# A linear-attention plus MoE kernel on one core: a new ramp, decays one unit earlier, and k and r transposed by the DMA

## The chip, the core and the metric

The kernel runs on one core of a Trainium2 chip. The metric is device time in microseconds (us) of the slowest core, here the only one. The engines are TensorE (PE in the profile, PEld for its weight loads), VectorE (DVE), ScalarE (ACT), GpSimd (POOL) and SyncE (SP), which here issues every DMA. Each engine executes its own instructions in the order in which the program gives them to it, as the traces show.

The kernel before has a median of 236.32 us over its first 3 runs (235.04 to 237.77).

## The reference, cut to what matters

The inputs r, k, v and w have the shape (4 batches, 8 heads, 768 steps, 48), in float32. The first part is a recurrence with a decaying state; the second is a dense layer pair with a gelu between.

```python
for t in range(S):                        # S = 768
    cur = einsum('bhd,bhe->bhde', u[None] * kt, vt)
    y[:, :, t] = einsum('bhd,bhde->bhe', rt, state + cur)
    state = wt[:, :, :, None] * state + einsum('bhd,bhe->bhde', kt, vt)
x = y.transpose(0, 2, 1, 3).reshape(B * S, H * D)      # 3072 x 384
h = x @ w_in                                           # 384 x 2048
g = 0.5 * h * (1 + tanh(c * (h + 0.044715 * h**3)))
out = g @ w_out                                        # 2048 x 384
```

## The kernel before

The work is cut into 12 units: 3 windows of 256 time steps times 4 batches. Inside a window the recurrence becomes matmuls. The logarithms of w are summed with triangular matrices on TensorE (`a1`), ScalarE takes exponentials of the sums (`exps`), VectorE multiplies k and r by them (`kk`, `rq`), and both products are transposed (`a2`) because the next matmuls contract over the head dimension. The term with u needs the row sum of r·k·u (`rk`, `dg`, `vsc`). Then the dense layer pair (called MoE in the program and below) runs on the unit's 256 rows (`mm1`, `mm2`). The attention of unit q+1 is woven into the MoE of unit q, and the preparation of unit q+2 follows it.

```python
def prep(q):                                    # cut
    DVE.tensor_tensor(out=kk[:, :, :, 0:D], in0=tdh(kt), in1=dec(e1), op=AL.mult)
    DVE.tensor_tensor(out=rq[:, :, :, 0:D], in0=tdh(rt), in1=dec(fq), op=AL.mult)
    POOL.tensor_copy(out=vb, in_=tdh(vt))
    POOL.tensor_tensor(out=rk, in0=kt..., in1=rt..., op=AL.mult)
    POOL.tensor_tensor(out=rk, in0=rk, in1=u_bc..., op=AL.mult)
    ...

def a2(q, which):
    src = (kk, rq)[which]
    for g in range(G):
        for t2 in range(2):
            PE.transpose(ps[:, g, :, t2, :], src[:, t2, ds(2 * g, 2), :], ident)
    DVE.tensor_copy(out=dst, in_=ps)

for q in range(NU):                             # the main loop, cut
    if q + 3 < NU:
        for nm in ("k", "r", "v"):
            load(q + 3, nm)                     # at the top, needed by prep(q+3) a unit later
    if q + 4 < NU:
        load(q + 4, "w")
    ...                                         # mm1, mm2, attention(q+1), a1(q+2)
    exps(q + 2)
    ln(q + 3)
    mm2(q, 0, range(12, 16))
    store(q, 0)
    prep(q + 2)
    prep_b(q + 2)
    mm2(q, 1, ...)
    store(q, 1)
```

In unit 0 the weights of w_out are cast to bfloat16 as well: all eight casts are placed before the first `mm2` and before most of the attention of unit 1.

Of the kernel before, what the change touches and what calls it, by code (L numbers as in the profile page):

```python
# [19 lines left out]
def kernel(  # L20
# [15 lines left out]
    P = 128  # L36
# [90 lines left out]
    kk_ps = [pfix.tile([P, 2, H, 64], BF, name=f"kk{i}") for i in range(2)]  # L127
    rq_ps = [pfix.tile([P, 2, H, 64], BF, name=f"rq{i}") for i in range(2)]
# [19 lines left out]

    st = {}
# [10 lines left out]
    def ln(q):  # L160
        lw = logws[q % 3]
        ACT.activation(  # L162
            out=lw[:, :, :, 0:D].rearrange("p t h d -> p h t d"),
            in_=ld.pop(("w", q)).rearrange("p h (t d) -> p h t d", t=2), func=AF.Ln)

    def a1(q):
        lw = logws[q % 3]
        x, y, z = (ps_a.tile([P, 512], FP, tag="a", name=f"cum{q}_{i}") for i in range(3))
        for dst, s0, s1 in ((x, strict, strict), (y, incl, strict), (z, incl, incl)):
            PE.matmul(dst[:, 0:HD], s0, lw[:, 0, :, 0:D], start=True, stop=False)  # L170
            PE.matmul(dst[:, 0:HD], s1, lw[:, 1, :, 0:D], start=False, stop=True)  # L171
        for g in range(G):
            for t2 in range(2):
                PE.matmul(z[:, ds(HD + 2 * g, 2)], lw[:, t2, ds(2 * g, 2), :], ones2,
                          start=False, stop=(t2 == 1), skip_group_check=True)
        st["cum", q] = (x, y, z)

    def exps(q):
        x, y, z = st.pop(("cum", q))
        fq = pw2.tile([P, 2, HD], BF, tag="fq", name=f"fq{q}")  # L180
        e1 = pw2.tile([P, 2, HD], BF, tag="e1", name=f"e1{q}")
        al = pw2.tile([P, G, 2], FP, tag="al", name=f"al{q}")
        ACT.activation(out=e1[:, 0, :], in_=y[:, 0:HD], func=AF.Exp, scale=-1.0)
        ACT.activation(out=e1[:, 1, :], in_=z[:, 0:HD], func=AF.Exp, scale=-1.0)
        ACT.activation(out=fq[:, 0, :], in_=x[:, 0:HD], func=AF.Exp)
        ACT.activation(out=fq[:, 1, :], in_=y[:, 0:HD], func=AF.Exp)
        ACT.activation(out=al, in_=z[:, ds(HD, 2 * G)].rearrange("p (g c) -> p g c", c=2),  # L187
                       func=AF.Exp)
        st["dec", q] = (fq, e1, al)

    def prep(q):
        fq, e1, al = st.pop(("dec", q))
        kt, rt, vt = ld.pop(("k", q)), ld.pop(("r", q)), ld.pop(("v", q))
        kk, rq = kk_ps[q % 2], rq_ps[q % 2]

        def tdh(ap):
            return ap.rearrange("p h (t d) -> p t h d", t=2)

        def dec(ap):
            return ap.rearrange("p t (h d) -> p t h d", h=H)  # L200

        DVE.tensor_tensor(out=kk[:, :, :, 0:D], in0=tdh(kt), in1=dec(e1), op=AL.mult)
        DVE.tensor_tensor(out=rq[:, :, :, 0:D], in0=tdh(rt), in1=dec(fq), op=AL.mult)  # L203
        vb = pw2.tile([P, 2, H, D], BF, tag="vb", name=f"vb{q}")
        POOL.tensor_copy(out=vb, in_=tdh(vt))
        rk = pw2.tile([P, H, 2, D], FP, tag="rk", name=f"rk{q}", bufs=1)
        dg = pw2.tile([P, H, 2], FP, tag="dg", name=f"dg{q}")
        vsc = pw2.tile([P, 2, H, D], BF, tag="vsc", name=f"vsc{q}")
        am = pw2.tile([P, 2, G, 2 * D], FP, tag="am", name=f"am{q}")
        POOL.tensor_tensor(out=rk, in0=kt.rearrange("p h (t d) -> p h t d", t=2),  # L210
                           in1=rt.rearrange("p h (t d) -> p h t d", t=2), op=AL.mult)
        POOL.tensor_tensor(out=rk, in0=rk,  # L212
                           in1=u_bc[:, :, None, :].broadcast_to([P, H, 2, D]), op=AL.mult)
        for c2 in range(2):
            POOL.tensor_tensor(  # L215
                out=am[:, c2], in0=blk.rearrange("p g j d -> p g (j d)"),
                in1=al[:, :, c2][:, :, None].broadcast_to([P, G, 2 * D]), op=AL.mult)
        st["pre", q] = (kk, rq, vb, vsc, am)
        st["diag", q] = (rk, dg)

    def prep_b(q):
        kk, rq, vb, vsc, am = st["pre", q]
        rk, dg = st.pop(("diag", q))
        DVE.tensor_reduce(out=dg, in_=rk, axis=AX.X, op=AL.add)
        POOL.tensor_tensor(
            out=vsc, in0=vb,
            in1=dg.rearrange("p h t -> p t h")[:, :, :, None].broadcast_to([P, 2, H, D]),
            op=AL.mult)

    def a2(q, which):  # L230
        kk, rq, vb, vsc, am = st["pre", q]
        src = (kk, rq)[which]
        ps = ps_a.tile([P, G, 2, 2, 64], BF, tag="a", name=f"T{q}_{which}")
        for g in range(G):
            for t2 in range(2):
                PE.transpose(ps[:, g, :, t2, :], src[:, t2, ds(2 * g, 2), :], ident)  # L236
        dst = pw2.tile([P, G, 2, 2, 64], BF, tag=f"T{which}", name=f"TT{q}_{which}")
        DVE.tensor_copy(out=dst, in_=ps)  # L238
        st["T", q, which] = dst

    def a3(q, rnd):
        kT, rT = st["T", q, 0], st["T", q, 1]
        mts = [ps_a.tile([P, 2, 2, P], FP, tag="a", name=f"mt{q}_{rnd}_{j}") for j in range(2)]
        for gi in range(2):
            g = 2 * rnd + gi
            for t2 in range(2):
                for j in range(2):
                    for c2 in range(2):
                        PE.matmul(mts[j][ds(64 * c2, 64), gi, t2, :],
                                  kT[ds(64 * j, D), g, c2, t2, :],  # L250
                                  rT[ds(64 * j, D), g, c2, :, :],
                                  start=(gi + t2 == 0), stop=(gi + t2 == 2))
# [8 lines left out]
    def a4(q):  # L261
        wi, b = units[q]
        kk, rq, vb, vsc, am = st["pre", q]
# [10 lines left out]
        for t2 in range(2):  # L274
            for c2 in range(2):
                rows = ds(64 * c2, 64)
                PE.matmul(ys[c2][:, :, :],
                          sel.rearrange("p a b t -> p a (b t)")[rows, t2, :],
                          vsc[rows, t2, :, :], start=False, stop=False,
                          skip_group_check=True)  # L280
        st["y", q] = ys

    def a4p(q):
        wi, b = units[q]
        kk, rq, vb, vsc, am = st["pre", q]
# [3 lines left out]
        for g in range(G):  # L289
            for t2 in range(2):  # L290
                for c2 in halves:
                    rows = ds(64 * c2, 64)
                    PE.matmul(p2[c2][:, g, :], kk[rows, t2, ds(2 * g, 2), :],
# [17 lines left out]
    def a5(q, c2):  # L311
        ys, rT = st["y", q], st["T", q, 1]
        s = st.pop(("S", q, c2))
        for g in range(G):
            if s is not None:
                PE.matmul(ys[c2][:, ds(2 * g, 2), :], rT[:, g, c2, :, :], s[:, g, :],
# [7 lines left out]
    def a6(q):  # L324
        xs = st.pop(("xs", q))
        ps = ps_a.tile([P, NCB, 2, P], BF, tag="a", name=f"xTp{q}")
        for c2 in range(2):
            for cb in range(NCB):
                PE.transpose(ps[:, cb, c2, :], xs[:, c2, ts(cb, P)], ident)
        xT = pw2.tile([P, NCB, WIN], BF, tag="xT", name=f"xT{q}")  # L330
        DVE.tensor_copy(out=xT, in_=ps.rearrange("p a b t -> p a (b t)"))
# [5 lines left out]
    def mm1(q, i):  # L337
# [4 lines left out]
        for f in range(2):  # L342
            ft = 2 * i + f
            for cb in range(NCB):
                PE.matmul(h[:, f, :], w_in_sb[:, cb, ts(ft, P)], xT[:, cb, :],  # L345
# [25 lines left out]
    def attention(q):  # L371
        a2(q, 1)
        a2(q, 0)
        yield
# [13 lines left out]

    for i in range(6):
        load_w_in(i)  # L390
    for nm in ("k", "r", "v"):
        load(1, nm)
# [6 lines left out]
    for nm in ("k", "r", "v"):  # L399
        load(2, nm)  # L400
# [3 lines left out]
    a1(0)  # L404
    exps(0)
    prep(0)
    ln(1)
    att = attention(0)
    next(att)
    next(att)  # L410
    next(att)
    prep_b(0)
    next(att)
    cast_w_in(0, ACT)
    cast_w_in(1, ACT)
    cast_w_in(2, DVE)
    next(att)
    next(att)
    next(att)
    cast_w_in(3, ACT)  # L420
    cast_w_in(4, POOL)
    cast_w_in(5, DVE)
    a1(1)
    exps(1)
    prep(1)
    prep_b(1)

    for q in range(NU):
        if q + 3 < NU:
            for nm in ("k", "r", "v"):  # L430
                load(q + 3, nm)
        if q + 4 < NU:
            load(q + 4, "w")
        att = attention(q + 1) if q + 1 < NU else iter(())
        table("gelu")
        ramp = q < 2
        if ramp:
            for i in range(8):
                mm1(q, i)
            if q == 0:  # L440
                for i in range(8):
                    cast_w_out(i, DVE if i in (0, 3, 6) else (ACT if i in (1, 4, 7) else POOL))
        for i in range(8):
            if not ramp:
                mm1(q, i)
            if i >= 2:
                mm2(q, 0, (2 * i - 4, 2 * i - 3))
            if i in (1, 3, 4, 5, 6, 7):
                next(att, None)
            if i == 6 and 0 < q and q + 2 < NU:  # L450
                a1(q + 2)
        table("exp")
        if q == 0:
            ln(2)
            a1(2)
        if q + 2 < NU:
            exps(q + 2)
        if q + 3 < NU:
            ln(q + 3)
        mm2(q, 0, range(12, 16))  # L460
        if not ramp:
            for _ in att:
                pass
        store(q, 0)
        if q + 2 < NU:
            prep(q + 2)
            prep_b(q + 2)
        mm2(q, 1, range(8))
        for _ in att:
            pass  # L470
        mm2(q, 1, range(8, 16))
        store(q, 1)

# [29 lines left out]
```

## Time and profile before

I measure a unit from the first MoE matmul of one unit (`h_0`) to that of the next, as the timeline shows them. "Start" is the time up to the first of them.

| us | start | unit 0 | 1 | 2 | 3 | 4 to 8 | 9, 10 | last | sum |
|---|---|---|---|---|---|---|---|---|---|
| before | 24.78 | 28.96 | 20.30 | 17.30 | 16.57 | 82.15 | 30.58 | 15.26 | 235.9 |

The page of the kernel before gives the busy time and share of each engine, then, for 40 equal slices of the span, the busy tenths of TensorE and the clock that it was granted (PEclk, in tenths of full speed).

```profile
span 235.9 us, 5759 instructions
...
PE 203.4 (86%) x2448; PEld 143.0 (61%) x2448; DVE 131.3 (56%) x211; ACT 134.0 (57%) x223; POOL 104.5 (44%) x87
...
PE   0456787598895999999999999999999999999992
...
PEclk9999996779997999999999999999999999999998
```

From about the fourteenth slice on, TensorE has no slack. Before that there is a ramp in which it is idle for part of most slices, and its clock falls to 0.6 or 0.7 in some of them.

The view of busy time by stretch shows the same for the start, unit 0 and a steady unit. Columns: the stretch, its length, busy us and instruction count of each engine, granted clock, DMA share (above 1 in some stretches, so not used here), GB/s.

```profile
core 0: us, PE busy (x) PEld busy (x) DVE busy (x) ACT busy (x) POOL busy (x), PEclk, DMA share, GB/s
0.00:24.78 24.78, 11.34 (x138) 7.68 (x139) 16.05 (x41) 9.32 (x14) 11.07 (x20) 1.00 1.04 294
24.78:53.74 28.96, 21.54 (x210) 13.49 (x207) 19.95 (x21) 16.41 (x27) 18.43 (x14) 0.82 0.80 212
124.47:141.03 16.56, 15.89 (x210) 11.42 (x208) 10.18 (x17) 10.51 (x20) 8.22 (x6) 1.00 0.54 121
```

In the steady unit TensorE is busy 15.89 of 16.56 us. VectorE is at 10.2, so there is room on every other engine.

The timeline of VectorE and GpSimd in unit 0 of the kernel before:

```profile
42.50 0.56 DVE L304 TENSOR_TENSOR tmp_1_642<-p_1_622,S_0_639 128x384 f32<-128x384 f32 x1
43.14 1.80 POOL L212 TENSOR_TENSOR rk_696<-rk_696,u_bc 128x768 f32<-128x768 f32 x1
43.16 2.20 DVE L305 TENSOR_TENSOR S_1_641<-tmp_1_642,am_421 128x384 bf16<-128x384 f32 x1
```

Two VectorE operations of the same shape follow each other. The first takes 0.56 us; the second, which reads two tiles from SBUF, the memory on the chip that the engines share, while a GpSimd instruction runs, takes 2.20 us and ends at 45.36, which is 0.42 us after the GpSimd instruction ended (44.94).

### The profile page before, as it was taken

How to read it: one execution, taken by the hardware profiler on the slowest of the kernel's cores; microseconds unless marked ns; L12 is line 12 of the kernel's file. 1: busy time of each engine (PE TensorE's matmuls, PEld its weight loads, DVE VectorE, ACT ScalarE, POOL GpSimd, SP SyncE). 2: the span in 40 equal slices, each digit the busy share in tenths (PEclk: the TensorE clock that was granted, in tenths of full speed). 3: DMA queues.
4: the chain of work that ended last, by engine and by line, in shares of the span. 5: the costliest groups of instructions: out<-in, count | busy, mean ns of one | idle time of the engine just before them, and what ended most of it. 6: DMA issues, size and time to landing. Idle time of an engine off the chain costs nothing.

```text
span 235.9 us, 5759 instructions
## 1 busy us (share of the span) xinstructions
PE 203.4 (86%) x2448; PEld 143.0 (61%) x2448; DVE 131.3 (56%) x211; ACT 134.0 (57%) x223; POOL 104.5 (44%) x87
## 2 busy tenths in 40 slices
PE   0456787598895999999999999999999999999992
PEld 0334564357564767667767667676777677677761
DVE  7684686561636538547547747656285376374200
ACT  3433780566255449459368377395494684765670
POOL 3473792639008504806708509329158076060000
PEclk9999996779997999999999999999999999999998
DMA  7999999713902911942923914915719120020202
GB/s 173 307 396 297 331 320 255 160 33 72 231 15 54 246 25 36 206 98 53 232 56 75 257 24 111 210 33 124 182 35 212 24 62 10 13 56 0 68 1 67
DMA packets 56969, 30.45 MB, mean 129 GB/s; under 512 B 50928, under 2 KB 56176, under 8 KB 56944
## 3 DMA queue, kind: packets, MB, share of 16 engines
q1 hardware_dynamic: 56944, 30.09, 52.1%
q8 instruction: 19, 0.31, 0.6%
q14 instruction: 6, 0.05, 0.1%
HBM read 25.36 MB, written 4.72 MB: 127 GB/s over the span
## 4 chain that ended last, share of the span: by engine, by line
PE 54%; ACT 19%; DVE 11%; issue 9%; POOL 3%; DMA 2%; DVEq 0%; ACTq 0%; POOLq 0%
ACT L156 5%; DVE w_out_sb L86 2%; DMA w_89<-in_w_dram 2%; PE o_0_532 L354 1%; DVE rq_127 L203 1%; ACT logw_124 L162 1%; PE o_0_3678 L354 1%; PE o_0_3457 L354 1%; PE o_0_3175 L354 1%; PE o_1_3740 L354 1%; PE o_1_3632 L354 1%; PE o_1_3389 L354 1%; POOL rk_418 L210 1%; POOL rk_418 L212 1%; ACT logw_122 L162 1%
## 5 line engine op out<-in xcount | busy, mean ns | idle before, releaser
L345 PEld LDWEIGHTS <-w_in_sb 128*128 128x128 bf16 x576 | 54.0, 99 | 21.1 <-issue 9.9
L156 ACT ACT_TABLE_LOAD x13 | 16.7, 1283 | 0.9 <-PEq L487 0.7
L158 ACT ACT_TABLE_LOAD x12 | 15.4, 1283 | 0.2
L171 PEld LDWEIGHTS <-strict 128*128 128x128 bf16 x24 | 2.5, 104 | 9.9 <-issue 9.5
L215 POOL TENSOR_TENSOR am_997<-blk,al_975 128x384 f32<-128x384 bf16 x2 | 2.4, 1230 | 12.5 <-ACT al_975 L187 12.5
L215 POOL TENSOR_TENSOR am_1304<-blk,al_1273 128x384 f32<-128x384 bf16 x2 | 2.4, 1229 | 11.5 <-ACT al_1273 L187 11.5
L215 POOL TENSOR_TENSOR am_1608<-blk,al_1577 128x384 f32<-128x384 bf16 x2 | 2.4, 1230 | 8.3 <-ACT al_1577 L187 8.3
L215 POOL TENSOR_TENSOR am_1912<-blk,al_1881 128x384 f32<-128x384 bf16 x2 | 2.4, 1230 | 8.3 <-ACT al_1881 L187 8.3
L215 POOL TENSOR_TENSOR am_2216<-blk,al_2185 128x384 f32<-128x384 bf16 x2 | 2.4, 1230 | 8.3 <-ACT al_2185 L187 8.3
L215 POOL TENSOR_TENSOR am_2520<-blk,al_2489 128x384 f32<-128x384 bf16 x2 | 2.4, 1228 | 8.3 <-ACT al_2489 L187 8.3
L215 POOL TENSOR_TENSOR am_2811<-blk,al_2780 128x384 f32<-128x384 bf16 x2 | 2.4, 1228 | 7.9 <-ACT al_2780 L187 7.9
L215 POOL TENSOR_TENSOR am_3100<-blk,al_3069 128x384 f32<-128x384 bf16 x2 | 2.4, 1228 | 7.9 <-ACT al_3069 L187 7.9
L215 POOL TENSOR_TENSOR am_3382<-blk,al_3352 128x384 f32<-128x384 bf16 x2 | 2.4, 1228 | 7.9 <-ACT al_3352 L187 7.9
L354 PE MATMUL o_0_532<-w_out_sb,g_437 128*128 128x384 bf16 x16 | 5.5, 469 | 0.2 <-ACT w_out_sb L84 0.2
L236 PEld LDWEIGHTS <-rq_127 128*128 128x128 bf16 x48 | 3.4, 104 | 3.3 <-DVE rq_127 L203 3.2
L354 PEld LDWEIGHTS <-g_437 128*128 128x128 bf16 x32 | 3.3, 117 | 3.2 <-issue 2.5
L170 PE MATMUL cum_0_201<-logw_122,strict 128*128 128x384 bf16 x1 | 0.5, 479 | 5.4 <-ACT logw_122 L162 5.4
L362 DVE COPY ob_3736<-o_0_3678 128x384 f32<-128x384 f32 x1 | 0.6, 558 | 7.7 <-PE o_0_3678 L354 7.7
L215 POOL TENSOR_TENSOR am_699<-blk,al_677 128x384 f32<-128x384 bf16 x2 | 2.3, 1187 | 4.3 <-ACT al_677 L187 4.3
L354 PEld LDWEIGHTS <-g_3653 128*128 128x128 bf16 x32 | 3.0, 98 | 1.7 <-ACT g_3653 L347 0.4
L238 DVE COPY TT_1_818<-T_1_809 128x1024 bf16<-128x1024 bf16 x1 | 0.7, 692 | 6.0 <-PE T_1_809 L236 6.0
L354 PE MATMUL o_0_3678<-w_out_sb,g_3653 128*128 128x384 bf16 x16 | 3.8, 327 | 0.0
(942 smaller groups left out, 694.2 us busy)
## 6 DMA issues: line engine op xcount, KB each, us to landing
wi_155<-in_moe_w_in_dram SPq DMA_DIRECT2D x1, 512.0 KB, 5.0
wi_157<-in_moe_w_in_dram SPq DMA_DIRECT2D x1, 512.0 KB, 6.0
wi_159<-in_moe_w_in_dram SPq DMA_DIRECT2D x1, 512.0 KB, 6.7
wi_161<-in_moe_w_in_dram SPq DMA_DIRECT2D x1, 512.0 KB, 7.5
wi_163<-in_moe_w_in_dram SPq DMA_DIRECT2D x1, 512.0 KB, 8.7
wi_165<-in_moe_w_in_dram SPq DMA_DIRECT2D x1, 512.0 KB, 9.6
w_89<-in_w_dram SPq DMA_DIRECT2D x1, 384.0 KB, 3.7
k_91<-in_k_dram SPq DMA_DIRECT2D x1, 384.0 KB, 4.7
```

The source lines that it names most:

```text
L86: eng.tensor_copy(out=out, in_=in_)
L156: ACT.preload_act_table_set(EXP_SET)
L158: ACT.preload_act_table(AF.Gelu_apprx_tanh)
L162: ACT.activation(out=lw[:, :, :, 0:D].rearrange("p t h d -> p h t d"), in_=ld.pop(("w", q)).rearrange("p h (t d) -> p h t d", t=2), func=A ...
L171: PE.matmul(dst[:, 0:HD], s1, lw[:, 1, :, 0:D], start=False, stop=True)
L203: DVE.tensor_tensor(out=rq[:, :, :, 0:D], in0=tdh(rt), in1=dec(fq), op=AL.mult)
L210: POOL.tensor_tensor(out=rk, in0=kt.rearrange("p h (t d) -> p h t d", t=2), in1=rt.rearrange("p h (t d) -> p h t d", t=2), op=AL.mult)
L212: POOL.tensor_tensor(out=rk, in0=rk, in1=u_bc[:, :, None, :].broadcast_to([P, H, 2, D]), op=AL.mult)
L215: POOL.tensor_tensor(out=am[:, c2], in0=blk.rearrange("p g j d -> p g (j d)"), in1=al[:, :, c2][:, :, None].broadcast_to([P, G, 2 * D]), o ...
L236: PE.transpose(ps[:, g, :, t2, :], src[:, t2, ds(2 * g, 2), :], ident)
L345: PE.matmul(h[:, f, :], w_in_sb[:, cb, ts(ft, P)], xT[:, cb, :], start=(f + cb == 0), stop=(cb == NCB - 1), skip_group_check=True)
L354: PE.matmul(st["o", q, c2], g[:, ft, ts(c2, P)], w_out_sb[:, ft, :], start=(ft == 0), stop=(ft == NFT - 1))
```

## The change

The intent was to take work off TensorE in the steady units and to shorten the ramp.

- The matmuls of one of three cumulative sums go away. Instead VectorE multiplies half of k and half of r by w (`prep_w`), and the two full multiplies `kk` and `rq` become four half-size ones.
- From the sixth unit (q = 5) on, `kk` and `rq` are transposed by DMA, not by TensorE. The MoE input is still transposed by TensorE.
- Decays are computed one unit earlier, so that unit q prepares unit q+3.
- The first three units get a loop of their own; the casts of w_out are spread between the attention steps of unit 1.
- The loads of k, r and v move with it: unit q+4 at the end of unit q.

```diff
-        DVE.tensor_tensor(out=kk[:, :, :, 0:D], in0=tdh(kt), in1=dec(e1), op=AL.mult)
-        DVE.tensor_tensor(out=rq[:, :, :, 0:D], in0=tdh(rt), in1=dec(fq), op=AL.mult)
+    def prep_w(q):
+        DVE.tensor_tensor(out=kw, in0=kt[:, :, 0:D], in1=wt[:, :, D:2 * D], op=AL.mult)
+        DVE.tensor_tensor(out=rw, in0=rt[:, :, D:2 * D], in1=wt[:, :, 0:D], op=AL.mult)
...
+        for dst, t2, x, dec in ((kk, 0, kw, e1), (kk, 1, kt[:, :, D:2 * D], e1),
+                                (rq, 0, rt[:, :, 0:D], fq), (rq, 1, rw, fq)):
+            DVE.tensor_tensor(out=dst[:, :, t2, :, 0:D], in0=gjd(x), in1=dec..., op=AL.mult)
...
+        for c2 in range(2):                        # a2, from unit 5 on (PE_T = (5, 5))
+            SP.dma_start(out=dst[:, c2]..., in_=src[ds(64 * c2, 64)]..., transpose=True)
...
+    for q in range(3):                             # the ramp, cut and condensed
+        for i in range(8): mm1(q, i)
+        wo(0); mm2(q, 0, (0, 1)); next(att); wo(1); mm2(q, 0, (2, 3)); next(att)
+        prep_b(1); wo(2); wo(3); mm2(q, 0, range(4, 8)); next(att); wo(4)
+        ...                                        # wo(i): cast i on ScalarE (even) or VectorE (odd), q == 0 only
+    for q in range(3, NU):                         # the steady loop, cut and condensed
+        n = q + 3
+        for i in range(8):
+            mm1(q, i)
+            if i == (4 if q == 3 else 0): prep_a(n)     # rk, vb on GpSimd
+            if i == 5: prep_w(n)
+            if i == 6: a1(n); prep_b(n)
+        exps(n); ln(q + 4); ...
+        store(q, 0)
+        prep(n)
+        for i in range(2):
+            if n >= PE_T[i]: a2(n, i)                   # the DMA transposes
+        mm2(q, 1, range(16))
+        store(q, 1)
+        krv(q + 4)                                      # loads of k, r, v
+        if q + 5 < NU: load(q + 5, "w")
```

Unit 3 prepares two units (5 and 6), to gain the extra step of lead.

## The prediction

> **What bounds it now.** The granted TensorE clock is 0.97 on average. The stage table (busy time per stretch) shows two regimes. From the fourth unit on, TensorE is the limit: in 129 to 161 us it is busy 15.33 of 16 us, while VectorE and ScalarE are at about 10 and GpSimd at 7.7. The first matmul of each unit's MoE phase, in the timeline, gives periods of 16.56 us (units 3 to 6), 16.23 (7 to 9), 14.35 (unit 10) and about 15.3 to the end. The ramp is the other regime: first MoE matmul at 24.78 us, then periods of 28.96, 20.30 and 17.30 us, so unit 3 starts at 91.34. There TensorE waits on a serial chain (loads, VectorE multiply, row sum, GpSimd vsc, sel matmuls) and on VectorE doing weight casts (31.5 to 35.4 us) ahead of the transposed copies; its clock is 0.82 in 24.8 to 53.7 us.
>
> **Steady state.** Removed from TensorE per unit:
> - The y cumulative sum: two 384-column matmuls at 0.163 us = 0.33 us.
> - From unit 5 on, 16 transposes at 0.056 us = 0.90 us (timeline: 142.34 to 143.24).
>
> Of the gaps (0.36 us before h_2 behind a late gelu, 0.31 us inside the sums behind xs) I expect about half to go: decays run earlier, and ScalarE loses two exps (about 0.38 us each). Periods should become about 15.9 (unit 3), 14.9 (units 4 to 6), 14.6 (7, 8) and 13.5 (9, 10); the last stays at 15.3. This sums to about 132 us for units 3 to 11 instead of 144.6: 12 us gained, all of it on the critical path because TensorE is the limit.
>
> VectorE is about neutral: it loses two copies (1.36 us) and two multiplies (1.9), and gains six half-size multiplies (estimate 0.56 each, as the 384-column ones now). The DMA gains four transposes, 512 KB a unit. The Trainium skill, "DMA: Bandwidth & Descriptors", Latency and other measured facts, gives 261 GB/s (about 350 to 400 contiguous), so an estimate of 1.3 to 2 us a unit. Loads take 54% of the engines now, and the attention that reads the result starts most of a unit later, so this should hide. No run here shows a DMA transpose yet.
>
> **Ramp.** The rk product no longer waits behind decays, the sums of unit 1 leave the path, and casts are spread between attention stages instead of standing in front of them. I expect the first MoE matmul at about 22.5 us. DMA runs at 90% to about 40 us and VectorE is nearly full there, so unit 0 still takes about 25 us, and units 1 and 2 about 18.5 and 18. Unit 3 then starts near 84 us: 7.5 us gained.
>
> **Time.** 236.3 - 12 - 7.5 = about 216.5 us, range 208 to 225. Chances: faster by over 2% 0.94, within 2% 0.04, slower by over 2% 0.02.
>
> **What would show it.** Steady period near 14.9 us in units 4 to 6; no transposes by TensorE there except xTp; wait of the a3 matmuls on the transposed tiles near zero; unit 3 starting at 81 to 87 us; granted clock in the ramp above 0.9.
>
> **What would make it wrong.** DMA transposes much slower than the skill's figure, or holding the SyncE queue so that stores and loads come late: periods then grow from unit 4 and matmuls wait on the transposed tiles. VectorE multiplies stretched by simultaneous GpSimd work (rq took 2.56 us instead of 0.95 at 26 us) could keep the ramp at its old length. A much better ramp, unit 0 in about 20 us, would bring 210.

## More of the kernel before

The timeline of SyncE's queue and of GpSimd (start, duration, engine, line, operation, out<-in):

```profile
75.68 0.54 SPq L69 DMA_DIRECT2D k_1033<-in_k_dram  x1
76.27 0.68 SPq L69 DMA_DIRECT2D r_1035<-in_r_dram  x1
...
95.27 0.82 POOL L205 CAST vb_1603<-v_1037 128x768 bf16<-128x768 f32 x1
96.06 1.81 POOL L210 TENSOR_TENSOR rk_1605<-k_1033,r_1035 128x768 f32<-128x768 f32 x1
```

k is issued at 75.68 and first read at 96.06. The load has 20 us, more than a whole unit, to land.

## The result and the profile after

The change made the kernel slower: 272.37 us median over 4 runs (271.61 to 273.52), against 236.09 (235.04 to 237.77) for the kernel before. The ratio is 1.1533, with a 95% interval of 1.1447 to 1.1619. Ratios here are the mean time of one kernel's fast runs over that of the other's of the same rounds, so they are not quite the ratio of the medians that I quote.

| us | start | unit 0 | 1 | 2 | 3 | 4 to 8 | 9, 10 | last | sum |
|---|---|---|---|---|---|---|---|---|---|
| before | 24.78 | 28.96 | 20.30 | 17.30 | 16.57 | 82.15 | 30.58 | 15.26 | 235.9 |
| predicted | 22.5 | 25 | 18.5 | 18 | 15.9 | 73.9 | 27.0 | 15.3 | 216.1 |
| after | 27.97 | 36.47 | 16.71 | 16.78 | 22.65 | 104.53 | 28.89 | 15.8 | 269.8 |

Against the prediction the sum is 53.7 us too long: 30.6 of it in units 4 to 8, 11.5 in unit 0, 6.8 in unit 3, 5.5 in the start, and 2.4 at the end. Units 1 and 2 are 3 us better than predicted. The same lines of the page and of the busy-time view, now of the kernel after:

```profile
span 269.8 us, 5526 instructions
...
PE 203.1 (75%) x2312; PEld 139.8 (52%) x2312; DVE 154.3 (57%) x247; ACT 127.0 (47%) x201; POOL 100.7 (37%) x84
...
PE   1274754559999899499929949929957976999992
...
PEclk9999985569999999689977997997995995999998
```

```profile
core 0: us, PE busy (x) PEld busy (x) DVE busy (x) ACT busy (x) POOL busy (x), PEclk, DMA share, GB/s
0.00:27.97 27.97, 10.67 (x135) 7.11 (x135) 21.05 (x45) 8.81 (x15) 14.74 (x21) 1.00 0.84 234
27.97:64.44 36.47, 23.44 (x215) 14.49 (x215) 15.84 (x24) 16.46 (x26) 10.57 (x9) 0.72 0.70 189
140.15:160.74 20.59, 16.49 (x191) 11.26 (x191) 11.90 (x19) 9.91 (x16) 8.38 (x7) 0.89 0.60 122
```

TensorE's rows say it at once: in the steady part a slice of 2, 4 or 5 stands between the nines, once per unit, where there was none before, and the clock dips with each. TensorE executes 136 matmuls fewer than before, but its busy time is the same (203.1 against 203.4), since it runs more of them at a lower clock (0.894 on average against 0.968). VectorE is busy 23 us longer, with work that was to be neutral.

What TensorE waits for in these holes is in the timeline. This is one turn of the loop in the kernel after, on SyncE's queue (SPq), GpSimd, VectorE and TensorE:

```profile
140.59 1.14 SPq L387 DMA_DIRECT2D out_dram<-ob_1948  x2
142.87 2.56 SPq L258 DMA_TRANSPOSE TT_0_1959<-kk_126  x2
145.53 2.52 SPq L258 DMA_TRANSPOSE TT_1_1962<-rq_129  x2
148.15 1.18 SPq L387 DMA_DIRECT2D out_dram<-ob_1948  x2
149.42 0.96 SPq L69 DMA_DIRECT2D k_1985<-in_k_dram  x1
150.43 0.56 SPq L69 DMA_DIRECT2D r_1987<-in_r_dram  x1
155.24 2.11 POOL L195 TENSOR_TENSOR rk_2004<-k_1985,r_1987 128x768 f32<-128x768 f32 x1 [11.75 <-DMA r_1987<-in_r_dram]
157.43 1.80 POOL L197 TENSOR_TENSOR rk_2004<-rk_2004,u_bc 128x768 f32<-128x768 f32 x1
159.27 0.95 DVE L206 TENSOR_REDUCE dg_2198<-rk_2004 128x16 f32<-128x768 f32 x1 [3.58 <-POOL rk_2004 L197]
160.14 0.55 DVE L353 COPY xT_2224<-xTp_2225 128x768 bf16<-128x768 bf16 x1
160.74 0.81 PE L367 MATMUL h_0_2284<-xT_2224,w_in_sb 128*128 128x256 bf16 x6 [3.98 <-DVE xT_2224 L353]
```

Read it downwards as one chain. SyncE issues a store, then holds its queue 5.1 us with four transposes, then the second store, and only then k and r, at 149.42 and 150.43. GpSimd has been waiting 11.75 us for r. It multiplies twice, VectorE sums the rows, and the copy of the next MoE input (`xT`), which has nothing to do with k or r but stands behind that sum on VectorE, comes after it. TensorE has waited 3.98 us for that copy. The next unit's multiplies, transposes and loads follow from there, so the loop closes on itself. What the transposes add to it can be read here: the copy that the second store sends off ended at 144.85 us (VectorE's timeline), and the store had to wait until 148.15, 3.3 us, for the queue. The same k that had 20 us to land before now has none to spare. The idle time in brackets names only the last link: "<-DVE xT" is the copy, while the cause is several steps earlier.

The transposes themselves were not late. The DMA view in the stretch from 140 to 160 us (issues, size, median us from issue to landing):

```profile
k_1985<-in_k_dram SPq DMA_DIRECT2D x1, 384.0 KB, 4.2
r_1987<-in_r_dram SPq DMA_DIRECT2D x1, 384.0 KB, 4.7
...
TT_0_1959<-kk_126 SPq DMA_TRANSPOSE x2, 2.8
TT_1_1962<-rq_129 SPq DMA_TRANSPOSE x2, 3.5
```

The timeline of the start of the kernel after shows VectorE and GpSimd taking turns:

```profile
7.58 1.85 POOL L195 TENSOR_TENSOR rk_226<-k_91,r_93 128x768 f32<-128x768 f32 x1 [4.87 <-DMA r_93<-in_r_dram]
7.80 2.05 DVE L187 TENSOR_TENSOR kw_236<-k_91,w_89 128x384 f32<-128x384 f32 x1
...
10.71 0.55 DVE L236 TENSOR_TENSOR kk_125<-k_91,e_231 128x384 bf16<-128x384 f32 x1
...
11.06 1.85 POOL L197 TENSOR_TENSOR rk_226<-rk_226,u_bc 128x768 f32<-128x768 f32 x1 [1.63 <-DMA u_bc<-in_u_dram]
11.18 2.15 DVE L236 TENSOR_TENSOR rq_128<-r_93,fq_230 128x384 bf16<-128x384 f32 x1
```

Both stretched multiplies end 0.42 us after the GpSimd instruction that they overlap (9.85 against 9.43, and 13.33 against 12.91), as in the kernel before. Their neighbour without an overlap takes 0.55 us.

And TensorE in unit 0 of the kernel after waits again and again for casts of w_out (three of five such lines, the others wait 1.95 and 1.31 us):

```profile
39.47 0.80 PE L376 MATMUL o_0_526<-w_out_sb,g_437 128*128 128x384 bf16 x2 [2.84 <-ACT w_out_sb L84]
42.69 0.80 PE L376 MATMUL o_0_526<-w_out_sb,g_437 128*128 128x384 bf16 x2 [1.85 <-DVE w_out_sb L86]
...
53.26 0.80 PE L376 MATMUL o_0_526<-w_out_sb,g_437 128*128 128x384 bf16 x2 [2.91 <-DVE w_out_sb L86]
```

### The profile page after: what moved, and what is told of

It is laid out like the page before. It is cut to its first block, busy times and chain, and to the rows that moved or that the text cites. A ratio compares the mean times of both kernels' runs of the same rounds, so it can differ in the third digit from the quotient of the medians.

```text
span 269.8 us, 5526 instructions
## 1 busy us (share of the span) xinstructions
PE 203.1 (75%) x2312; PEld 139.8 (52%) x2312; DVE 154.3 (57%) x247; ACT 127.0 (47%) x201; POOL 100.7 (37%) x84
## 4 chain that ended last, share of the span: by engine, by line
PE 28%; DVE 10%; DMA 10%; POOL 7%; SPq 5%; issue 3%; ACT 0%; DVEq 0%; POOLq 0%; ACTq 0%
DMA r_2276<-in_r_dram 2%; DMA r_1698<-in_r_dram 2%; SPq L387 2%; DMA r_2565<-in_r_dram 2%; DMA r_1987<-in_r_dram 2%; DMA r_2841<-in_r_dram 2%; DVE kk_127 L236 2%; SPq L258 1%; SPq L69 1%; PE o_1_3642 L376 1%; PE o_1_3534 L376 1%; PE o_1_3313 L376 1%; PE o_1_1676 L376 1%; PE o_0_3596 L376 1%; PE o_0_3417 L376 1%
## 5 line engine op out<-in xcount | busy, mean ns | idle before, releaser
L367 PEld LDWEIGHTS <-w_in_sb 128*128 128x128 bf16 x576 | 57.2, 105 | 42.2 <-issue 27.0
L376 PE MATMUL o_0_526<-w_out_sb,g_437 128*128 128x384 bf16 x16 | 6.3, 507 | 10.9 <-DVE w_out_sb L86 6.7
L376 PEld LDWEIGHTS <-g_437 128*128 128x128 bf16 x32 | 3.2, 108 | 14.0 <-issue 12.9
L207 POOL TENSOR_TENSOR vsc_575<-vb_424,dg_574 128x768 bf16<-128x768 bf16 x1 | 1.7, 1664 | 15.8 <-DVE dg_574 L206 15.8
L195 POOL TENSOR_TENSOR rk_2293<-k_2274,r_2276 128x768 f32<-128x768 f32 x1 | 2.1, 2109 | 13.2 <-DMA r_2276<-in_r_dram 13.2
L195 POOL TENSOR_TENSOR rk_1715<-k_1696,r_1698 128x768 f32<-128x768 f32 x1 | 2.1, 2107 | 12.9 <-DMA r_1698<-in_r_dram 12.9
L195 POOL TENSOR_TENSOR rk_2582<-k_2563,r_2565 128x768 f32<-128x768 f32 x1 | 2.1, 2110 | 12.5 <-DMA r_2565<-in_r_dram 12.5
L195 POOL TENSOR_TENSOR rk_2856<-k_2839,r_2841 128x768 f32<-128x768 f32 x1 | 2.1, 2110 | 12.2 <-DMA r_2841<-in_r_dram 12.2
L195 POOL TENSOR_TENSOR rk_2004<-k_1985,r_1987 128x768 f32<-128x768 f32 x1 | 2.1, 2112 | 11.7 <-DMA r_1987<-in_r_dram 11.7
L367 PE MATMUL h_0_2573<-xT_2513,w_in_sb 128*128 128x256 bf16 x6 | 1.4, 413 | 5.5 <-DVE xT_2513 L353 5.5
L367 PE MATMUL h_0_1995<-xT_1935,w_in_sb 128*128 128x256 bf16 x6 | 1.4, 410 | 5.1 <-DVE xT_1935 L353 5.1
L367 PE MATMUL h_0_2847<-xT_2789,w_in_sb 128*128 128x256 bf16 x6 | 1.4, 413 | 4.7 <-DVE xT_2789 L353 4.7
L207 POOL TENSOR_TENSOR vsc_1336<-vb_1323,dg_1335 128x768 bf16<-128x768 bf16 x1 | 1.5, 1483 | 9.3 <-DVE dg_1335 L206 9.3
L367 PE MATMUL h_0_3114<-xT_3062,w_in_sb 128*128 128x256 bf16 x6 | 1.4, 413 | 4.3 <-DVE xT_3062 L353 4.3
L376 PEld LDWEIGHTS <-g_1368 128*128 128x128 bf16 x32 | 3.5, 109 | 1.9 <-issue 0.5
L241 POOL TENSOR_TENSOR am_753<-blk,al_691 128x384 f32<-128x384 bf16 x2 | 1.6, 830 | 7.5 <-ACT al_691 L220 7.5
```

Of the source, the lines that this page charges most:

```text
L195: POOL.tensor_tensor(out=rk, in0=kt.rearrange("p h (t d) -> p h t d", t=2), in1=rt.rearrange("p h (t d) -> p h t d", t=2), op=AL.mult)
L207: POOL.tensor_tensor(out=vsc, in0=vb, in1=dg.rearrange("p h t -> p t h")[:, :, :, None].broadcast_to([P, 2, H, D]), op=AL.mult)
L241: POOL.tensor_tensor(out=am[:, c2], in0=blk.rearrange("p g j d -> p g (j d)"), in1=al[:, :, c2][:, :, None].broadcast_to([P, G, 2 * D]), o ...
L367: PE.matmul(h[:, f, :], w_in_sb[:, cb, ts(ft, P)], xT[:, :, cb, :], start=(f + cb == 0), stop=(cb == NCB - 1), skip_group_check=True)
L376: PE.matmul(st["o", q, c2], g[:, ft, ts(c2, P)], w_out_sb[:, ft, :], start=(ft == 0), stop=(ft == NFT - 1))
```

## The experiments

All twelve runs gave correct results. They ran in several batches, each with its own runs of the kernel before, whose medians were 235.6 to 237.5 us.

### Is it the loads or the transposes?

My theory after reading the trace was that the position of the loads costs the time in units 4 to 8. The rival was that the DMA transposes themselves do, by holding the queue or by loading the DMA engines. Two edits, alone and together, make a square of four.

**loads_first.** The loads keep their place in SyncE's order, but bring the data of one unit later, so each has a whole unit more to land.

```diff
     for q in range(3, NU):
+        krv(q + 4)
+        if q + 5 < NU:
+            load(q + 5, "w")
         att = attention(q + 1) if q + 1 < NU else iter(())
...
         store(q, 1)
-        krv(q + 4)
-        if q + 5 < NU:
-            load(q + 5, "w")
```

> Edit: in the loop over units 3 to 11 the loads of k, r, v (four units ahead) and w (five ahead) stand at the top of the unit instead of at its end. Theory A (late loads: issued behind both stores and four transposes on the SyncE queue, needed at once by the next unit): periods of units 4 to 8 fall from 19.6 to 22.1 us to about 15, the waits of rk on r (12 us each) and of the MoE input's copy behind them go, total about 240 us. Rival B (the DMA transposes themselves are too slow or come too late): periods stay above 19 us, total above 265 us. Rival C (VectorE has too much work): in between, VectorE busy above 90% in those units.

Measured: 236.59, 240.82, 240.86 and 240.66 us. By the rule that a run more than 1.5% above the fastest counts as slow, only the first is fast; see loads_first_5 below. The profile is of the fast one. Units 4 to 8 fall from 104.5 to 72.5 us. The busy-time view of a steady unit and the timeline of the loads and their reader:

```profile
core 0: us, PE busy (x) PEld busy (x) DVE busy (x) ACT busy (x) POOL busy (x), PEclk, DMA share, GB/s
149.93:164.08 14.15, 14.15 (x192) 10.32 (x190) 11.24 (x19) 9.79 (x17) 8.46 (x7) 1.00 0.89 176
```

```profile
156.37 0.54 SPq L69 DMA_DIRECT2D k<-in_k_dram  x1
156.97 0.66 SPq L69 DMA_DIRECT2D r<-in_r_dram  x1
...
164.93 2.12 POOL L195 TENSOR_TENSOR rk<-k,r 128x768 f32<-128x768 f32 x1
```

TensorE is busy 14.15 of 14.15 us. k has 8.5 us from issue to first read, and GpSimd no longer waits for it. The DMA transposes are all still there.

**pe_transposes.** All transposes back on TensorE, loads still late.

```diff
-    PE_T = (5, 5)
+    PE_T = (12, 12)
```

> Edit: the change as it is, with all transposes of k and r on TensorE, loads left at the end of the unit. Theory A: the loop through the queue loses only its 5.1 us of transposes (20.6 to about 15.5 us), while TensorE gains 0.9 us a unit, so periods become 16 to 17 us, total about 247 us, and waits of rk on r remain, shorter. Rival B: all waits on loads go as well, periods about 15.8 us.

Measured: 259.77 us (259.01 to 262.16), ratio to before 1.0999 (1.0921 to 1.1077): slower. Units 4 to 8 take 89.6 us, in periods of 16.4 to 19.8 us where 16 to 17 were expected, and the total is 13 us above the expected 247. GpSimd still waits 8.0 us for r. k is now issued 5.4 us after the first MoE matmul of a unit (160.29 against 154.85); with the DMA transposes it was 9.3 us (149.42 against 140.15).

**loads_first_pe.** Both edits.

> Edit: both of the two above. It shows what the DMA transposes are worth once the loads are early: theory A expects periods of units 4 to 8 about 0.9 us above those of the run with early loads alone (15.8 against 14.9), so 5 to 6 us more in total, about 246 us. Rival B expects this run to be the fastest of the three.

Measured: 249.39 us (248.77 to 251.67), ratio 1.0545 (1.0476 to 1.0614): slower. A steady unit takes 15.77 us:

```profile
155.01:170.78 15.77, 15.12 (x208) 11.21 (x206) 12.44 (x21) 9.79 (x17) 8.45 (x7) 1.00 0.56 126
```

The square, in us of units 4 to 8 together:

| | loads late | loads a unit earlier | late loads cost |
|---|---|---|---|
| DMA transposes | 104.5 | 72.5 | 32.1 |
| TensorE transposes | 89.6 | 81.0 | 8.6 |
| DMA transposes cost | +15 | −8.5 | |

Each cell is one profiled run. The medians of the totals agree: early loads are worth 34.8 us with DMA transposes and 10.4 us without (loads_first_5 below stands for loads_first).

So the two don't add up. With the loads in time, the DMA transposes save 8.5 us in five units, more than the prediction gave them. With late loads they cost 15 us, 3 us a unit, and the traces say why: they stand in front of the loads in the queue (the 3.3 us above, and k issued at 9.3 instead of 5.4 us). No run put the transposes on another queue or behind the loads. The rival is wrong as a cause by itself and right as half of an interaction. What has to be repaired is the place of the loads.

### Unit 0: loads of the weights, or the order of their casts?

**own_stage.** In the kernel after, w_out is loaded into the staging tiles of w_in, so its loads wait for the casts of w_in (first issue 26.58 us; 19.10 before). Reading R1 says that this is why unit 0 is long. Reading R2 says that it is the order of the casts: each stands behind an attention step on an in-order engine, the next matmuls stand behind the cast, and the next attention step behind those matmuls. The edit, on loads_first, gives w_out tiles of its own and pays for the space with fewer buffers elsewhere.

```diff
-        t = pstage.tile([P, 2, HD], FP, tag=f"wi{i}", name=f"wo{i}")
+        t = pstage.tile([P, 2, HD], FP, tag={5: "wi2"}.get(i, f"wo{i}"), name=f"wo{i}")
```

> Edit: early loads, and the w_out transfers get staging buffers of their own instead of those of w_in (room from single kw, rw, tmp and three k, r, v buffers), so that they need not wait for the w_in casts, which the change placed late (first w_out issue at 26.6 us, 19.1 before). Theory R1 (unit 0 takes 36.5 us because the w_out transfers come late): unit 0 falls to about 30 us, total 6 us below early loads alone. Theory R2 (unit 0 is long because the in-order queues of TensorE, VectorE and ScalarE wait on each other in turn: each w_out cast stands behind an attention step and the next matmuls stand behind that cast): w_out issues move to about 20 us but unit 0 stays within 2 us of 36.5.

Measured: 237.31 us (236.78 to 239.51), ratio 1.0035 (0.9972 to 1.0098). The first load of w_out is now issued at 18.95 us, but unit 0 takes 36.82 us, and TensorE's waits for the casts are unchanged (2.84, 1.85, 1.95, 2.91 and 1.31 us). R1 falls.

**wo_ahead.** On loads_first: the eight casts in front of the attention, spread over three engines, as in the kernel before.

```diff
         if q == 0:
-            wo(0)
+            for i in range(8):
+                cast_w_out(i, DVE if i in (0, 3, 6) else (ACT if i in (1, 4, 7) else POOL))
         mm2(q, 0, (0, 1))
         next(att)
-        if q == 0:
-            wo(1)
...                                       # wo(2) to wo(7) likewise
```

> Edit: early loads, and in unit 0 all eight w_out casts stand ahead of the attention steps, three on VectorE, three on ScalarE, two on GpSimd (the order of the kernel before), instead of one behind each attention step. Theory R2 (TensorE, VectorE and ScalarE wait on each other in turn because each cast stands behind an attention step and the next matmuls behind that cast): unit 0 falls from 35.8 to about 29 us, the TensorE waits on w_out_sb (about 11 us in all) mostly go, total about 229 us. Rival R3 (unit 0 is long for another reason: clock, late starts of attention): within 2 us of 35.8.

Measured, two runs: 230.53 and 231.78 us, ratio 0.98 (0.9734 to 0.9866), which is "unclear" at the 2% border. Unit 0 takes 29.06 us instead of 35.77, and one wait of 1.9 us is left of TensorE's waits for casts. The granted clock in unit 0 rises from 0.72 to 0.88. The busy-time view of unit 0 in loads_first and in wo_ahead:

```profile
27.97:63.74 35.77, 22.75 (x215) 14.13 (x215) 15.85 (x24) 16.49 (x26) 10.58 (x9) 0.72 0.72 192
28.22:57.28 29.06, 22.14 (x214) 14.27 (x214) 14.44 (x23) 15.86 (x25) 12.05 (x11) 0.88 0.88 236
```

R2 holds; the intent of spreading the casts was the mistake. The edit also moves two casts to GpSimd; that this is not what helps is made likely by combined2 below, where no cast is on GpSimd, most stand ahead, and unit 0 takes 28.97 us.

### Unit 3

**unit3.** On loads_first: the multiplies of unit q+2 go to the top of units 1 and 2, with loads at the top throughout, so that unit 5 can be prepared in unit 2 and unit 3 prepares only one unit.

```diff
     for q in range(3):
+        krv(q + 4)
+        load(q + 5, "w")
...
+        if q > 0:
+            prep_w(q + 2); prep_a(q + 2); prep(q + 2)      # was after store(q, 0)
...
         store(q, 0)
+        if q == 2:
+            prep_w(5); prep_a(5); prep(5); a2(5, 0); a2(5, 1); prep_b(5)    # was in unit 3
```

> Edit: early loads in all units; the multiplies of unit q+2 stand at the top of units 1 and 2 instead of at their end, and those of unit 5 at the end of unit 2 instead of in the middle of unit 3. Theory U (unit 3 takes 22.7 us because it prepares two units, 5 and 6, and the state update of unit 4 stands behind unit 5's multiplies and row sum on VectorE, which GpSimd stretches): unit 3 falls to 14.5 to 16 us, unit 4 to 14.2, units 1 and 2 rise by at most 1 us, total about 227 us. Rival: unit 3 stays above 20 us, or units 1 and 2 take over what it loses.

Measured, two runs: 238.02 and 236.39 us, ratio 1.0056 (0.9984 to 1.0128). This is a miss. Unit 3 fell only from 22.68 to 20.97 us; unit 4 gained 1.7 us, unit 1 lost 2.1 us, and unit 0, of which only the loads were changed, lost 2.5 us (see u_first). In unit 3 TensorE now waits 4.29 us for the copies of the transposes of unit 4, which stand on VectorE behind the multiplies of unit 5. The work had been moved into the way of another one.

### The start

**start_order.** On loads_first: the cast of v of unit 0 goes to the front of GpSimd's work, off ScalarE, and the sums of unit 1 go behind the first masked matmuls.

```diff
+        if q == 0:
+            cast(POOL, vb, tdh(vt))
         POOL.tensor_tensor(out=rk, in0=kt..., in1=rt..., op=AL.mult)
...
-    a1(1, ps_h, "h")
     next(att)
     next(att)
+    a1(1, ps_h, "h")
```

> Edit: early loads, and before the first unit the order of the kernel before comes back in two places: GpSimd casts v before it multiplies k by r (so that this multiply starts 1.5 us later and VectorE multiplies undisturbed), ScalarE no longer casts v ahead of the first exps, and the sums of unit 1 come after the a3 matmuls of unit 0. Theory: the first MoE matmul was late (27.97 us instead of 24.78) because GpSimd's multiplies stretched VectorE's (kw 2.05 us instead of 0.54, rq 2.15 and 1.18 instead of 0.55), because exps(0) stood behind the cast of v, and because the sums of unit 1 stood in front of a3 (1.7 us). Expected: first MoE matmul at 24 to 25.5 us, everything after it unchanged. If it stays above 27 us the theory is wrong.

Measured, two runs: 238.68 and 238.53 us, ratio 1.0116 (1.0056 to 1.0176). A miss: the start moved from 27.97 to 27.45 us only, and unit 0 grew from 35.8 to 38.3 us. `kw` was now free (0.56 us), but one `kk` took 1.18 and both `rq` 2.16 and 2.15 us. GpSimd's instructions had been delayed onto the later multiplies.

**u_first.** On loads_first: r·u first and then ·k. GpSimd then waits for u, which arrives late (11.1 us), and by then VectorE has finished its multiplies. The cast of v stays on ScalarE, behind the exponentials. The sums of unit 1 move as in start_order.

```diff
-        POOL.tensor_tensor(out=rk, in0=kt..., in1=rt..., op=AL.mult)
-        POOL.tensor_tensor(out=rk, in0=rk, in1=u_bc..., op=AL.mult)
+        POOL.tensor_tensor(out=rk, in0=rt..., in1=u_bc..., op=AL.mult)
+        POOL.tensor_tensor(out=rk, in0=rk, in1=kt..., op=AL.mult)
...
     exps(0)
+    cast(ACT, st["a", 0][0], tdh(ld["v", 0]))
```

> Edit: early loads, and before the first unit GpSimd multiplies r by u first and then by k (u lands last, at about 11 us, so GpSimd starts only then), ScalarE casts v after the first exps, and the sums of unit 1 come after a3. Theory X (a VectorE multiply with two inputs from SBUF and a GpSimd instruction take turns, each waiting until the other's whole instruction has ended: in the traces every stretched multiply ends 0.42 us after the GpSimd instruction that it overlaps, and the last run only moved the GpSimd work onto the rq multiplies): kw, rw, kk and rq all take 0.55 us, rq ends at about 10.7 us instead of 14.4, the first MoE matmul is at 23 to 24.5 us instead of 27.97. Rival: the multiplies are slow for another reason (size, types, DMA writes at the same time): rq stays above 1.1 us and the first MoE matmul above 26.5 us.

Measured, two runs: 235.5 and 233.69 us, ratio 0.992 (0.9848 to 0.9992). The start is 22.54 us; the prediction had said 22.5. The timeline (first, an early and the last multiply, then GpSimd):

```profile
7.80 0.56 DVE L187 TENSOR_TENSOR kw<-k,w 128x384 f32<-128x384 f32 x1
...
10.15 0.55 DVE L237 TENSOR_TENSOR rq<-rw,fq 128x384 bf16<-128x384 f32 x1
...
11.13 1.81 POOL L195 TENSOR_TENSOR rk<-r,u_bc 128x768 f32<-128x768 f32 x1 [8.42 <-DMA u_bc<-in_u_dram]
```

The last multiply ends at 10.70, before GpSimd begins, and all six take 0.55 or 0.56 us. But of the 5.4 us gained only 1.1 reach unit 1, because unit 0 grew from 35.8 to 40.1 us. It has the same waits for casts in the same lengths, and the traces place the growth elsewhere. 2.5 us of it lie before the first of these waits, which ends 13.8 us after the start of the unit instead of 11.3: there the six multiplies of unit 1 now meet GpSimd (two take 2.2 us and three 1.2, where five of six took 0.55), and TensorE's transposes wait 1.3 us for them. The turns had been moved, not removed. 1.8 us lie at the end: the stretch from 54.0 us to the first MoE matmul of unit 1 takes 8.6 us at a granted clock of 0.58, where loads_first takes 6.8 us at 0.88 (from 56.9 us). start_order and unit3 have the same slow end (8.2 and 8.4 us at 0.61 and 0.60), so it doesn't come from this edit alone; what sets that clock is open.

### Putting the repairs together

**combined.** wo_ahead, start_order and unit3, with all casts of w_in on ScalarE and the casts of w_out split as VectorE two, GpSimd three, ScalarE three.

> Edit: the three above together, all six w_in casts on ScalarE in its idle time before the first attention output, and the w_out casts two on VectorE, three on GpSimd, three on ScalarE. A candidate to beat both kernels. Expected: first MoE matmul at about 23 us, unit 0 about 24 us, units 1 and 2 about 17 us, unit 3 about 15, units 4 to 8 14.2; total about 212 us. Above 225 us one of the parts doesn't add up with the others.

Measured: 224.02 us median (222.98 to 226.43), ratio 0.9483 (0.9432 to 0.9534): faster, but 12 us above the expected 212. The profiled run (226.43) was slow, and I use its periods only for where the time stands: start 27.3, unit 0 27.2, unit 3 21.7 us.

**combined2.** u_first, with most casts of w_out on ScalarE ahead of its table switch; the multiplies of unit 3 after the first store of unit 1, and the attention of unit 4 begun before the multiplies of unit 5, which are done in unit 3.

```diff
+            att4 = attention(4)
+            next(att4)
             prep_w(5)
             prep_a(5)
...
+            if q == 3 and i == 4:
+                prep(5); a2(5, 0); a2(5, 1); prep_b(5)
```

> Edit: the combined run, with the start of the other run of this call; the w_out casts one and then two on VectorE and five on ScalarE, none on GpSimd; unit 3 multiplies at the end of unit 1 again; unit 4's at the top of unit 2; the TensorE transposes of unit 4 and their copies ahead of unit 5's first products, and the rest of unit 5's multiplies behind the state update in unit 3. Expected: first MoE matmul at 23 to 24.5 us, unit 0 about 25 us, unit 1 16.7, unit 2 16.8, unit 3 about 17 instead of 21.7; total 212 to 217 us. Rival: unit 3 stays above 20 us, because GpSimd's work for units 5 and 6 and not the order on VectorE holds it.

Measured: 228.33 us (226.75 to 229.37), ratio 0.9633 (0.9579 to 0.9688): faster than the kernel before, but worse than combined and 11 us above the expected range. The start is 22.54 and unit 3 18.6 us, but unit 2 takes 23.7 and unit 4 18.1. In unit 2 TensorE waits 4.68 us for the transposed copies of unit 3. At the end of unit 3 it waits 4.27 us for the MoE input of unit 4, on VectorE behind a row sum that waited 5.02 us for GpSimd: the same last links as in the late-load loop. In unit 4 itself TensorE is busy 17.05 of 18.06 us, at a granted clock of 0.85.

**combined3.** Of each the better half: the order of combined for units 1 and 2 and for the casts, the start of u_first, unit 5 prepared in unit 2 but the attention of unit 4 begun before its multiplies. The sums of unit 3 stand in the middle of the second half of unit 0's `mm2`. The diff is cut, and against combined2.

```diff
         store(q, 0)
         if q == 2:
             att4 = attention(4)
             next(att4)
             prep_w(5)
             prep_a(5)
+            prep(5)
+            a2(5, 0)
+            a2(5, 1)
+            prep_b(5)
-        mm2(q, 1, range(16))
+        mm2(q, 1, range(8))
+        if q == 0:
+            a1(3)
+            exps(3)
+        mm2(q, 1, range(8, 16))
```

> Edit: the combined run (unit 2 prepared as there), with the undisturbed start of the run before (r by u first), v of unit 1 cast ahead of GpSimd's multiplies, unit 4's TensorE transposes and their copies ahead of unit 5's multiplies at the end of unit 2, and the sums of unit 3 behind the first half of unit 0's second output. Theory (turns between VectorE and GpSimd, and order on VectorE): first MoE matmul at 22.5 us, unit 0 at most 28 us, unit 3 17 to 18 us instead of 21.7 because the 4.3 us wait of the a3 matmuls on the transposed copies goes; total 214 to 218 us against 222 to 224. If unit 3 stays at 21 us or more, the wait has only moved to the masked copies, and VectorE's stretched multiplies of unit 5 and not their place before or behind the copies are the limit.

Measured: 215.8 us median (214.91 to 216.95), ratio 0.9114 (0.9022 to 0.9206): faster, and inside the expected 214 to 218. It beats both kernels. The busy-time view of unit 0 and unit 3:

```profile
22.53:47.11 24.58, 20.36 (x215) 13.75 (x214) 13.00 (x20) 12.90 (x24) 17.34 (x14) 0.93 1.13 297
83.61:102.12 18.51, 16.34 (x191) 11.37 (x190) 15.01 (x23) 9.36 (x16) 11.54 (x10) 0.91 0.68 124
```

Unit 0 has the clock at 0.93 and takes 24.58 us; the prediction had said about 25. Unit 3 still has 15.0 us of VectorE work and 2.2 us without TensorE.

**loads_first_5.** loads_first again, in five rounds, because its first batch had split into two groups.

> The same kernel as the run with early loads alone, whose four runs split into one at 236.6 us and three at 240.7 to 240.9 us, so that it got no verdict. Nothing new is expected of the units from 3 on. If the split is a property of the kernel, these runs show both values again and the profile that falls on the longer one shows it in units 0 to 2 (granted clock); if it was a disturbance of that chip, all runs lie within 1% of one value.

Measured: 237.59 us median, 237.34 to 239.12 over six runs, ratio 1.0023 (0.997 to 1.0076). So the one edit that moves the loads takes the kernel from 15% slower to even. The split into 236.6 and 240.7 us did not come back. Its cause is open; the granted clock of the slower group (0.941) was not below that of the faster run (0.923).

## Why the prediction was wrong

The periods of the two kernels that answer it, beside the prediction:

| us | start | unit 0 | 1 and 2 | 3 | 4 to 8 | 9, 10 | last | sum |
|---|---|---|---|---|---|---|---|---|
| predicted | 22.5 | 25 | 36.5 | 15.9 | 73.9 | 27.0 | 15.3 | 216.1 |
| after | 27.97 | 36.47 | 33.49 | 22.65 | 104.53 | 28.89 | 15.8 | 269.8 |
| loads_first | 27.97 | 35.77 | 33.50 | 22.68 | 72.46 | 26.60 | 15.82 | 234.8 |
| combined3 | 22.53 | 24.58 | 36.50 | 18.51 | 70.76 | 26.61 | 15.71 | 215.2 |

1. **"so this should hide" (steady state) was the step that failed, and it cost most.** The prediction checked where the results of the transposes are read, most of a unit later, and that was right. It did not check what stands behind them in SyncE's order: the loads of k, r and v, which the diff had moved to the end of the unit whose successor reads them at once. It named the danger ("holding the SyncE queue so that stores and loads come late") in its last paragraph but gave all of "slower" 0.02. It also expected such a loss to show as matmuls waiting on the transposed tiles; they waited on the MoE input, several links further on. The 20 us of lead in the trace before would have shown that lead was something to lose. Measured: 32.1 us in units 4 to 8, and moving the loads by one unit brings it back. The page "DMA: Bandwidth & Descriptors" of the Trainium skill, in its Rules for kernel authors, says to issue a DMA early and to wait for its semaphore late; this agrees, with 11.75 us of waiting against none.

2. **The size of the DMA transposes was underestimated, without harm by itself.** The estimate from the skill's 261 GB/s, and 350 to 400 for contiguous data, was 1.3 to 2 us a unit. They hold the queue 5.1 us in the unit shown, which for 512 KB is about 103 GB/s. With the loads early TensorE waits for nothing in such a unit (busy 14.15 of 14.15 us).

3. **The gain in TensorE was right, and somewhat better.** "Steady period near 14.9 us in units 4 to 6" became 14.15 once the loads were in time (15.85 in unit 4), and 13.3 in units 9 and 10 against 13.5. The square gives 8.5 us in five units to the DMA transposes, 1.7 us each; the prediction had counted 0.9. The two steady units shown above divide it: TensorE's busy time falls from 15.12 to 14.15 us, about the 0.9 that was counted, and the 0.65 us for which it waited behind a gelu go too. The prediction had expected about half of such gaps to go; why all of it went was not tested.

4. **"VectorE is about neutral", with six half-size multiplies of 0.56 each, was wrong under overlap.** The size holds when GpSimd is quiet, as u_first shows six times. When GpSimd runs, a multiply takes 1.18 to 2.16 us. The page "SBUF — State Buffer" of the Trainium skill, in its section SBUF: two separate sides, states why: VectorE and GpSimd share a pair of ports as an exclusive lock, and a VectorE operation with two SBUF inputs against a GpSimd operation that reads SBUF "fully blocks" until the first to start has finished. The traces agree: three times the end was 0.42 us after GpSimd's. I had not looked this up before I predicted, though I had seen one such line (2.56 us) and written it down as a risk. By that account two large multiplies can lose two turns, six small ones six; here three of six lost one. That is most of the start: 27.97 us, and 22.54 without the overlap and with the sums of unit 1 and the cast of v out of the way.

5. **"casts are spread between attention stages instead of standing in front of them", and so unit 0 takes about 25 us, was wrong in sign.** Spread over in-order engines, each cast waits for an attention step that waits for TensorE, which waits for the previous cast. Five waits of 1.3 to 2.9 us and a clock of 0.72 made it 36.5 us. wo_ahead brought 6.7 us by undoing it. That the first half hung on the lateness of the loads was my rival reading, and own_stage refuted it.

6. **Unit 3 was not looked at.** It prepares two units, with 22 us of VectorE work as stretched in this trace, and takes 22.65 us instead of 15.9. Its work can be moved (18.5 us in combined3), not removed. In combined3, units 1 and 2 pay 3.0 us for it.

7. **The sum was reachable.** combined3, with the same arithmetic and the same transposes as the change and another order of instructions, has unit 3 starting at 83.61 us (predicted 84) and takes 215.8 us (predicted 216.5). This does not make the prediction right: it was made about this program, and it costed the work but not the order.

What stays open: the split of the first batch of loads_first; what lowers the clock at the end of unit 0 in u_first, start_order and unit3; and why units 1 and 3 stay at 18.8 and 18.5 us in combined3, where I read waits behind VectorE but tried no further order.

## What to carry to other kernels

When a change puts work on an in-order queue, list what stands behind that work in the queue and when its reader needs it; asking only when the new work's own result is read misses the cost. Look up, for each load, the time from issue to first read in the trace before, and see what the change leaves of it. When a VectorE operation with two SBUF inputs is split into small ones, count how many of them will overlap GpSimd, and give each of those up to the length of the GpSimd instruction.

## What the Trainium skill lacked or had wrong

- "DMA: Bandwidth & Descriptors" has no time for how long a DMA transpose holds the queue of the engine that issues it on this chip; it has only sequencer cycles of "previous generations", in a comparison with trn3 B0. Here two transposes of 64×1024 two-byte elements, SBUF to SBUF, held SyncE's queue 2.5 to 3.9 us (median 2.54), and the issues behind them waited. Its 261 GB/s, in Latency and other measured facts, is a rate of data; these small ones come to 103 GB/s over the time that the queue is held.
- The same page's statement, in Rules for kernel authors, that a transpose next to ordinary DMAs needs nothing agrees: all runs with DMA transposes between loads and stores were correct. It speaks of correctness, not of time, and time is what it cost here: 15 us in five units with late loads.
- "GPSIMD Engine Reference", in Specifications, names contention with VectorE instructions that have two SBUF inputs, but not that the loser waits for the whole instruction; that is on the SBUF page. Here it made 0.55 us into as much as 2.16 us for VectorE, and 1.81 into 2.11 us for a GpSimd instruction that began 0.11 us after a VectorE one. No page warns that splitting one VectorE operation into small ones multiplies the turns that can be lost.
- "VectorE: DVE Perf Modes", in The three transpose paths, gives 1309 ns for one 128×128 block by DMA. No run here shows one block by itself; a block of 64×1024, four times the elements, held the queue for 1.26 us in the median (1.19 to 2.62).
